# Sinkhorn attention followed by a SwiGLU FFN: attention pieces threaded through the FFN in written order, the transposing V copies moved to ScalarE, and unread matmuls in TensorE's early gaps

## The chip, the cores and the metric

One core of a Trainium2 chip. The time is device time in microseconds, the median of several executions.

Engine names: PE is TensorE's matmuls and PEld its weight loads, DVE is VectorE, ACT is ScalarE, POOL is GpSimd. PSUM is the memory into which this kernel's matmuls write; a drain is a copy out of it. A unit is the attention of two heads over four blocks (scores, Exp, AV, division, transpose); a batch has eight, and four of them make the input of one FFN half.

## The reference

Four batches, eight heads, 768 tokens, head size 64; an FFN from 512 to 1536 and back over 3072 tokens.

```python
P = sort_net                                     # (4, 8, 8, 8)
for _ in range(5):                               # Sinkhorn
    P = exp(P - max(P, -1));  P /= sum(P, -1) + 1e-9;  P /= sum(P, -2) + 1e-9
k_sorted = einsum('bhij,bhjcd->bhicd', P, k_blocks)      # 8 blocks of 96 tokens
v_sorted = einsum('bhij,bhjcd->bhicd', P, v_blocks)
attn = softmax(q_block @ k_sorted.T / 8)                 # within each block
x = (attn @ v_sorted)                                    # -> (3072, 512)
g = x @ w_gate
out = (g * sigmoid(g) * (x @ w_val)) @ w_out
```

## The kernel before

K, Q and V arrive with (head, block) on the partitions, so that the sorting is a matmul by a small mixing matrix made from P. For V the weights of such a matmul are all 96 tokens of one d, which lie 64 elements apart in the loaded tile. So V is first copied into `vch`, with d and token exchanged:

```python
def emit_vch(pair):                                  # 4 copies, 128 partitions x 1536
    for s in range(4):
        cs = slice(s * (C // 4), (s + 1) * (C // 4))
        eng = nc.gpsimd if pair else nc.vector
        eng.tensor_copy(vch[:, :, cs], nat[:, cs, :].transpose([0, 2, 1]))

def emit_att(b):
    kqt = emit_kq(b)                     # 12 chunks of 16 matmuls, PSUM drained by DVE and ACT in turn
    ...                                  # 8 units: scores, Exp, AV, divide, transpose
            if b % 2 == 0: vts[b // 2] = emit_v(b // 2)      # V of two batches at once

emit_att(0)
for b in range(B):
    if b + 1 < B:
        emit_att(b + 1)
    emit_gv(b, 0); emit_gv(b, 1)         # FFN: gate and value, per half batch (384 tokens)
    emit_out(b, 0); emit_out(b, 1)
```

The FFN step for one 128-wide slice m of the hidden layer ties three engines together. The four `g_ps` and four `v_ps` matmuls need PSUM buffers ("gen", three of them), which come free only after ScalarE's tanh and VectorE's two multiplications:

```python
th_sb = tanh(g_ps / 2)                    # ACT
gs_sb = (th_sb + 1) * g_ps                # DVE
h     = (v_ps * 0.5) * gs_sb              # DVE
```

The order on every engine is the scheduler's.

The softmax here doesn't subtract the row's maximum and nothing guards it: scores larger than these inputs give would overflow.

## Time and profile before

| | |
|---|---|
| time | 285.56 us when the prediction was made, 285.91 us with a fourth run (the profile is of one of 287.63 us, span 285.9) |
| TensorE busy | 90% of the span |
| first `h` begun (last step of the first FFN slice) | 45.64 us |
| half-rate TensorE clock after 35 us | 17.1 us |
| gaps of TensorE over 0.3 us after 35 us | 2.5 us |

The page's busy times and, of its rows of 40 equal slices, those of TensorE and ScalarE and of the granted clock (in tenths; 5 is half rate), kernel before:

```profile
PE 257.2 (90%) x2600; PEld 152.7 (53%) x2608; DVE 178.9 (63%) x383; ACT 121.7 (43%) x246; POOL 39.1 (14%) x51
...
PE   0077799969999999999999999999999999999993
...
ACT  2036745437633215976534215764332134343211
...
PEclk9999955979999999999999999999999999999999
```

TensorE is full from slice 10 on. What could be won lies in front: hardly a matmul in the first two slices, then thin ones, then slices at half clock. The chain of waits of the kernel before, as shares of the span by engine:

```profile
PE 82%; DVE 11%; ACT 3%; issue 2%; ACTq 0%
```

In stretches (columns: stretch; its length and PE busy; then PEld, DVE, ACT and POOL busy with instruction counts; granted clock; DMA share and GB/s), kernel before:

```profile
35.60:49.20 13.60, 13.36 (x116) 7.14 (x111) 7.24 (x17) 6.50 (x15) 2.94 (x6) 0.50 1.13 209
57.40:59.90 2.50, 0.00 (x0) 0.00 (x0) 0.42 (x1) 0.06 (x1) 0.00 (x0) 0.93 1.04 213
...
65.00:100.00 35.00, 34.90 (x307) 20.64 (x307) 26.61 (x56) 16.39 (x37) 10.60 (x4) 1.00 0.25 56
```

The first FFN work runs at clock 0.50, and a later pause waits for a load (Q's second half for batch 1 landed at 59.60 us, and TensorE went on at 59.90). The transposing copies of the kernel before, by group and form (line, engine, operation, count; then busy us and mean ns; then idle time before them):

```profile
L204 POOL COPY vch<-v 128x1536 bf16<-128x1536 bf16 x4 | 11.2, 2878 | 0.0
...
L204 DVE COPY vch<-v 128x1536 bf16<-128x1536 bf16 x4 | 6.0, 1490 | 0.0
```

### The profile page before, as it was taken

To read this page: it belongs to the slowest core of one execution; us is meant where nothing else is said; L and a number is where in the kernel's file an instruction comes from. 1 tells how busy PE (TensorE), PEld (TensorE's weight loads), DVE (VectorE), ACT (ScalarE), POOL (GpSimd) and SP (SyncE) were. 2 spreads that over 40 slices of the span, in tenths; PEclk is the share of its full clock that TensorE was granted. 3 is DMA by queue.
4 is the path that set the end of the run, shared out by engine and by line. 5 is a ranking of instruction groups with operands and counts; after the bars stand their busy time and mean duration, and the time that the engine had idled before them with its cause. 6 is when DMAs were issued, how large, how long until landed. Compare 5 with 4: busy or idle time off the path is not lost.

```text
span 285.9 us, 6221 instructions
## 1 busy us (share of the span) xinstructions
PE 257.2 (90%) x2600; PEld 152.7 (53%) x2608; DVE 178.9 (63%) x383; ACT 121.7 (43%) x246; POOL 39.1 (14%) x51
## 2 busy tenths in 40 slices
PE   0077799969999999999999999999999999999993
PEld 0066555746655446666655446666555445555441
DVE  6798746937988205789988304699885018888300
ACT  2036745437633215976534215764332134343211
POOL 8557421029500000000000000000000000000000
PEclk9999955979999999999999999999999999999999
DMA  6999999999100122000000122000000220000021
GB/s 99 198 203 197 200 213 204 220 214 214 38 0 1 39 110 76 2 2 0 3 0 2 38 110 76 2 2 2 0 0 2 111 102 10 0 0 3 37 110 73
DMA packets 13659, 20.84 MB, mean 73 GB/s; under 512 B 1088, under 2 KB 8768, under 8 KB 13632
## 3 DMA queue, kind: packets, MB, share of 16 engines
q0 software_dynamic: 10128, 14.16, 28.2%
q1 hardware_dynamic: 3504, 6.30, 5.8%
q8 instruction: 20, 0.33, 0.4%
q14 instruction: 7, 0.06, 0.1%
HBM read 28.32 MB, written 6.29 MB: 121 GB/s over the span
## 4 chain that ended last, share of the span: by engine, by line
PE 82%; DVE 11%; ACT 3%; issue 2%; ACTq 0%
PE v_ps L297 22%; PE g_ps L288 22%; PE o_ps L308 22%; PE av_ps L245 4%; PE qk L230 4%; PE tkq L193 3%; PE x_ps L255 3%; PE tv L214 3%; DVE kqt L180 2%; DVE vch L204 1%; DVE st L251 1%; ACT vt L182 1%; DVE vt L180 1%; ACT th_sb L291 1%; DVE colred L136 0%
## 5 line engine op out<-in xcount | busy, mean ns | idle before, releaser
L288 PE MATMUL g_ps<-xt,wg_sb 128*128 128x384 bf16 x384 | 84.8, 331 | 0.2 <-DVE h L299 0.2
L297 PE MATMUL v_ps<-xt,wv_sb 128*128 128x384 bf16 x384 | 82.1, 331 | 0.0
L291 ACT ACTIVATE th_sb<-g_ps 128x384 bf16<-128x384 f32 x96 | 47.1, 491 | 63.2 <-PE g_ps L288 62.6
L293 DVE SCALAR_TENSOR_TENSOR gs_sb<-th_sb,g_ps 128x384 bf16<-128x384 bf16 x96 | 52.9, 551 | 26.9 <-ACT th_sb L291 20.9
L308 PE MATMUL o_ps<-wo_sb,h 128*128 128x512 bf16 x280 | 62.4, 379 | 0.4
L299 DVE SCALAR_TENSOR_TENSOR h<-v_ps,gs_sb 128x384 bf16<-128x384 f32 x96 | 53.1, 553 | 9.0 <-PE v_ps L297 0.8
L297 PEld LDWEIGHTS <-wv_sb 128*128 128x128 bf16 x384 | 36.8, 98 | 24.5 <-issue 0.8
L288 PEld LDWEIGHTS <-wg_sb 128*128 128x128 bf16 x384 | 36.2, 99 | 23.5 <-issue 2.3
L308 PEld LDWEIGHTS <-h 128*128 128x128 bf16 x288 | 28.2, 98 | 33.6
L180 DVE CAST kqt<-tkq 128x512 bf16<-128x512 f32 x24 | 15.9, 688 | 33.9 <-PE tkq L193 33.9
L311 ACT COPY o_sb<-o_ps 128x512 f32<-128x512 f32 x24 | 14.1, 586 | 51.4 <-PE o_ps L308 51.4
L235 ACT ACTIVATE er<-qk 96x384 bf16<-96x384 f32 x64 | 27.1, 487 | 12.2 <-PE qk L230 12.2
L193 PE MATMUL tkq<-rmix,kq 128*64 128x64 bf16 x768 | 20.3, 212 | 5.5 <-issue 2.5
L193 PEld LDWEIGHTS <-kq 128*64 128x64 bf16 x768 | 17.7, 126 | 8.9 <-issue 7.9
L251 DVE TENSOR_TENSOR st<-av_ps,r_sb 96x512 bf16<-96x512 f32 x32 | 21.9, 684 | 0.8
L182 ACT CAST kqt<-tkq 128x512 bf16<-128x512 f32 x24 | 14.1, 586 | 15.7 <-PE tkq L193 15.6
L230 PE MATMUL qk<-kqt 64*128 64x96 bf16 x256 | 14.0, 217 | 1.9 <-DVE kqt L180 1.4
L245 PE MATMUL av_ps<-vt,er 96*128 96x65 bf16 x256 | 14.9, 202 | 0.2 <-ACT vt L182 0.2
L180 DVE CAST vt<-tv 96x512 bf16<-96x512 f32 x16 | 12.2, 785 | 2.7 <-PE tv L214 2.5
L182 ACT CAST vt<-tv 96x512 bf16<-96x512 f32 x16 | 12.5, 787 | 2.1 <-PE tv L214 1.8
L214 PE MATMUL tv<-vmix,vch 128*128 128x128 bf16 x128 | 12.4, 236 | 1.0 <-DVE vt L180 0.3
L255 PEld LDWEIGHTS <-st 96*128 96x128 bf16 x128 | 7.6, 101 | 10.5 <-DVE st L251 9.1
(43 smaller groups left out, 123.0 us busy)
## 6 DMA issues: line engine op xcount, KB each, us to landing
out_dram<-o_sb SPq DMA_DIRECT2D x24, 256.0 KB, 2.0
v<-in_v_dram POOLq DMA_DIRECT2D x8, 384.0 KB, 13.1
kq<-in_k_dram POOLq DMA_DIRECT2D x6, 384.0 KB, 11.6
kq<-in_q_dram POOLq DMA_DIRECT2D x6, 384.0 KB, 12.1
wg_sb<-in_moe_w_gate_dram POOLq DMA_DIRECT2D x6, 256.0 KB, 11.8
wv_sb<-in_moe_w_val_dram POOLq DMA_DIRECT2D x6, 256.0 KB, 11.1
wo_sb<-in_moe_w_out_dram POOLq DMA_DIRECT2D x1, 1536.0 KB, 18.9
kq<-in_k_dram POOLq DMA_DIRECT2D x4, 192.0 KB, 5.6
```

Of the source, the lines that this page charges most:

```text
L180: nc.vector.tensor_copy(dst, src)
L182: nc.scalar.copy(dst, src)
L193: nc.tensor.matmul(tp[two * D:(two + 1) * D, lc, :], lhsT=nat[:, cb * 8 + lc, :], rhs=rm[:, two, :], start=True, stop=True)
L230: nc.tensor.matmul(pss[two][:, i4, :], lhsT=flat[lo:lo + D, at:at + 128], rhs=kqt[lo:lo + D, 1, g, i, :], start=True, stop=True)
L235: nc.scalar.activation(e[:, 0:4 * C], pss[two][0:C].rearrange("p a c -> p (a c)"), AF.Exp, scale=scale)
L245: nc.tensor.matmul(av[:, two, i4, :], lhsT=es[two][:, i4 * C:i4 * C + 128], rhs=vt[:, 2 * g + two, half * 4 + i4, :], start=True, stop=True)
L288: nc.tensor.matmul(g_ps, lhsT=wg_sb[:, kc, ts(m, 128)], rhs=xt[:, kc, :], start=(kc == 0), stop=(kc == NKC - 1))
L291: nc.scalar.activation(th_sb, g_ps, AF.Tanh, scale=0.5)
L293: nc.vector.scalar_tensor_tensor(gs_sb, th_sb, 1.0, g_ps, op0=ALU.add, op1=ALU.mult)
L297: nc.tensor.matmul(v_ps, lhsT=wv_sb[:, kc, ts(m, 128)], rhs=xt[:, kc, :], start=(kc == 0), stop=(kc == NKC - 1))
L299: nc.vector.scalar_tensor_tensor(h_w[:, m, :], v_ps, 0.5, gs_sb, op0=ALU.mult, op1=ALU.mult)
L308: nc.tensor.matmul(o_ps, lhsT=h_w[:, m, ts(t3, 128)], rhs=wo_sb[:, m, :], start=(m == 0), stop=(m == NFC - 1))
```

## The change

Its intent is to start the FFN as soon as half of batch 0 is through attention, to spread the rest of attention over the first seven of the eight FFN halves so that TensorE always has dense work, and to keep its clock up by matmuls that nobody reads. All engines follow the written order in the prologue; TensorE and GpSimd also do so afterwards. The core of the diff (cut):

```diff
+    man = tc.manual_schedule(engines={ET.PE, ET.Pool, ET.DVE, ET.Activation})
     for it in range(N_ITER):
         nc.scalar.activation(p_sb, p_sb, AF.Exp)
+        if it >= 2:
+            copy_v(nc.scalar, 0, lowr, it - 2)      # vch copy, 64 x 1536, between two Exp
 ...
+    copy_v(nc.scalar, 0, lowr, 3)
+    warm(lowr, v_tiles[0]..., 4); warm(highr, kq_tiles[0]..., 4); warm(both, kq_tiles[0]..., 5)
+    ...                                             # w_ps, V of batch 0 alone (8 chunks), K/Q (12)
+    for u in range(4):                              # 4 of 8 units, with 16 unread matmuls between
+        qk(0, u); warm(both, kqts[0][:, 0:512], 2, warm_ps)
+        ...
+    man = tc.manual_schedule(engines={ET.PE, ET.Pool})
+    def copies(pair, rows, count):
+        return [(0.0, lambda s=s: copy_v(nc.scalar, pair, rows, s, count)) for s in range(count)]
+    merge(ffn(0), units(0, range(4, 8)) + mingle(kqs(1), copies(0, highr, 8)))
+    merge(ffn(1), [v_chunk(1, db, "s", "att") ...] + units(1, range(4)))
+    merge(ffn(2), mingle(units(1, range(4, 8)) + kqs(2), copies(1, slice(0, 128), 8)))
+    merge(ffn(3), [v_pair_chunk(1, db, "s", "att") ...] + units(2, range(4)))
+    merge(ffn(4), units(2, range(4, 8)) + kqs(3))
+    merge(ffn(5), units(3, range(4)));  merge(ffn(6), units(3, range(4, 8)));  merge(ffn(7), [])
-    emit_att(0) ... emit_gv ... emit_out            # the loop shown above
```

`merge` puts a few pieces of attention after each FFN slice. `ffn(n)` holds the 12 slices of half n and the output matmuls of half n-1.

## The prediction

> **What bounds it now.** TensorE. The page's busy table gives PE 90% of the span, and the chain of waits is 82% PE, nearly all FFN matmuls. Read by stages (windows, timeline), the 285.9 us are:
>
> - 0 to 36.0: PE does no FFN work. Sinkhorn ends at 11.9, first attention matmul 14.4; VectorE spends 6.0 us on four vch copies (1.49 us each) inside the kq stage, and both batches' V are mixed (16 drains of 0.79 us) before FFN starts.
> - 35.6 to 49.2 and 59.8 to 62.5: granted clock 0.50; consecutive 128x384 matmuls start 0.32 us apart instead of 0.163. Half of 16.3 us is lost, about 8 us. The Trainium skill (TensorE: Matmul & The Clock Gate, Part 1) says that an idle window drops the clock to half; this trace agrees: PE was 8% busy at 34-35 and idle at 57.4-59.9.
> - 57.4 to 59.9: PE idle ("issue"), batch 1's second K/Q half not landed: 2.5 us.
> - From there PE is nearly full; after the last matmul (281.3) 4.6 us of drain and store.
>
> Warm costs from the timeline: one FFN half 23.6 us (12 x 1.32 + 3 x 2.58), all eight 189; one attention unit (scores, AV, transpose) 0.80 us of PE; one kq chunk 0.29 to 0.36 us; V mixing 3.5 to 4 us per pair. Estimate of PE work after FFN start: about 229 us.
>
> **What changes.** (1) vch copies go to ScalarE (four of about 1.4 us, in Sinkhorn's gaps); V of batch 0 alone is mixed first, in 8 chunks. (2) FFN starts after four units instead of after the whole of batch 0; all other attention work is threaded between FFN groups in written order, its drains mostly on ScalarE. (3) 13 early unread matmuls plus about 17 between the first units keep the clock up. They cost some PE time, mostly in waits. The work in total is unchanged; only place and clock are.
>
> **New prologue (estimate).** Loads run at about 0.2 MB/us bf16 (windows): V0 lands near 7, K/Q 0 near 15.4. Early unread matmuls end near 13; w_ps about 13.5; V chunks 14.4 to 17.6; kq 17.6 to 22.5; four units, paced by VectorE (0.20+0.68+0.36 us) and start-up latency, about 7 us: FFN starts near 30, warm.
>
> **Sum.** 30 + 229 + 4.6 = 264. Add 6 to 7 us: in FFN half 0 ScalarE has about 24 us of work (12 tanh, 8 exp, 12 kq drains, 8 copies) against 23 us of PE, and V of batch 1 lands only near 42.6, so ScalarE's copies may hold up tanh; elsewhere PE in written order waits now and then for a drain. Prediction 270 us, range 262 to 278. Gain: 6 us earlier start, 8 clock, 2.5 stall, less deferred and new waits.
>
> **What would show it.** FFN's first g_ps near 30 (right) or after 33 (wrong). No 0.50 clock after FFN starts; kq chunks at 20-23 us near 21 ns a matmul, not 31. PE 97% busy or more from 30 on. If ScalarE binds, waits of g_ps or tkq for ScalarE (copies, tanh) show in FFN half 0, between 36 and 46. FFN halves 5 to 7 at 27 us or less.
>
> **What would make it wrong.** The clock falls anyway (unread matmuls too sparse, or a stall near 40 us): +4 to 7. ScalarE's copies wait for V inside Sinkhorn and delay it. In-order PE blocks on drains at each of some 150 threaded pieces: 0.1 us each is 15 us, which would leave the gain below 2%. If none of that happens, 263.
>
> Chances: faster 0.90, same 0.08, slower 0.02.

## The result and the profile after

The changed kernel takes 295.10 us (four runs, 294.79 to 296.67) against 285.91: ratio 1.033, 95% interval 1.028 to 1.039. It is slower, where 270 us was expected.

The same parts of the page, changed kernel:

```profile
PE 260.2 (89%) x2701; PEld 149.1 (51%) x2701; DVE 154.3 (53%) x351; ACT 162.7 (55%) x281; POOL 18.6 (6%) x34
...
PE   0867975599988799899989998999999999999994
...
ACT  4976459976599645454887444455443353333311
...
PEclk9999999789999799999999999999999999999999
...
PE 76%; ACT 14%; DVE 5%; issue 3%; DMA 1%; ACTq 0%
```

TensorE is no fuller than before. In slices 7 and 8 and again around 12 and 13 it has holes, and there ScalarE is at 9. In the chain of waits ScalarE rose from 3% to 14%. The groups show what it does there:

```profile
L111 ACT COPY vch<-v 128x768 bf16<-128x768 bf16 x8 | 12.0, 1538 | 0.0
L111 ACT COPY vch<-v 64x768 bf16<-64x768 bf16 x8 | 11.6, 1497 | 0.1
...
L111 ACT COPY vch<-v 64x1536 bf16<-64x1536 bf16 x4 | 11.1, 2786 | 0.0
```

The prediction had 1.4 us for the 1536-element copy; it takes 2.79, nearly twice what VectorE took before. How this hurts is seen in time order in the prologue, ScalarE alone (columns: start, duration, engine, line, operation; in brackets the idle time before it and what ended it):

```profile
5.95 0.26 ACT L163 ACTIVATE p_sb<-p_sb 32x64 f32<-32x64 f32 x1 [1.50 <-DVE p_sb L177]
6.13 2.80 ACT L111 COPY vch<-v 64x1536 bf16<-64x1536 bf16 x1
8.83 0.25 ACT L163 ACTIVATE p_sb<-p_sb 32x64 f32<-32x64 f32 x1
8.99 2.78 ACT L111 COPY vch<-v 64x1536 bf16<-64x1536 bf16 x1
11.67 0.25 ACT L163 ACTIVATE p_sb<-p_sb 32x64 f32<-32x64 f32 x1
11.83 5.48 ACT L111 COPY vch<-v 64x1536 bf16<-64x1536 bf16 x2
```

The gap between two Exp was 1.50 us, so a copy of 2.8 delays each following Exp, and the last copy ends at 17.3. TensorE waits for it before V's first matmul:

```profile
14.11 0.61 PE L349 MATMUL w_ps<-ident,p_bf 32*64 32x32 bf16 x16
...
17.36 0.87 PE L232 MATMUL tv<-vmix,vch 64*128 64x64 bf16 x13 [2.64 <-ACT vch L111]
```

And in FFN half 0, all engines between 47.5 and 53.2 us (weight loads left out):

```profile
47.58 4.29 ACT L111 COPY vch<-v 64x768 bf16<-64x768 bf16 x3
...
49.02 0.82 PE L307 MATMUL g_ps<-xt,wg_sb 128*128 128x384 bf16 x4
...
51.89 0.49 ACT L310 ACTIVATE th_sb<-g_ps 128x384 bf16<-128x384 f32 x1
...
52.41 0.56 DVE L312 SCALAR_TENSOR_TENSOR gs_sb<-th_sb,g_ps 128x384 bf16<-128x384 bf16 x1 [4.18 <-ACT th_sb L310]
...
53.02 0.65 PE L316 MATMUL v_ps<-xt,wv_sb 128*128 128x384 bf16 x3 [3.17 <-DVE gs_sb L312]
```

The gate matmuls end near 49.8. Their tanh has to stand behind a row of copies on ScalarE until 51.9; VectorE waits for the tanh, the PSUM buffer stays taken, and TensorE stands still for 3.17 us. Soon after, from 54.4 to 61.3 us, the trace's clock records show half rate. The Trainium skill (TensorE: Matmul & The Clock Gate, Part 1) says that an idle window of the activity monitor does that; both half-rate stretches after 35 us (the other is 98.8 to 102.2) follow holes here. But the stretches before them were not empty: the lengths of these clock records are multiples of 3.41 us, and in the last 3.41 us before each drop TensorE was busy for 1.42 and 1.38 us.

Three of TensorE's longest waits in the changed kernel, by place (columns: who waited for whom; us in total, times, longest):

```profile
PE v_ps L316 <- DVE gs_sb L312: 6.1, 4, 3.2
PE av_ps L277 <- DVE st L283: 6.1, 6, 1.4
...
PE g_ps L307 <- ACT o_sb L329: 2.2, 1, 2.2
```

The first and the last lead to ScalarE, by way of the tanh and of the output's drain (one of the four at v_ps, 1.4 us, stays when the copies leave ScalarE); the second is another matter, as rival B below says.

For a comparison of all kernels I use three numbers that I worked out from each trace: when the first `h` is begun, the sum of TensorE's gaps over 0.3 us after 35 us, and the half-rate time after 35 us.

| | time | first h | gaps | half rate |
|---|---|---|---|---|
| before | 285.9 | 45.6 | 2.5 | 17.1 |
| changed | 295.1 | 37.4 | 15.3 | 10.2 |

So the change did start the FFN earlier, by 8 us at the first `h`, and part of the half-rate time went. But work is deferred with that, and 13 us of new gaps follow.

### The profile page after: what moved, and what is told of

It reads as the page before. It is cut to its first block, busy times and chain, and to the rows that moved or that the text cites. A ratio compares the mean times of both kernels' runs of the same rounds, so it can differ in the third digit from the quotient of the medians.

```text
span 293.6 us, 6359 instructions
## 1 busy us (share of the span) xinstructions
PE 260.2 (89%) x2701; PEld 149.1 (51%) x2701; DVE 154.3 (53%) x351; ACT 162.7 (55%) x281; POOL 18.6 (6%) x34
## 4 chain that ended last, share of the span: by engine, by line
PE 76%; ACT 14%; DVE 5%; issue 3%; DMA 1%; ACTq 0%
PE o_ps L326 21%; PE g_ps L307 20%; PE v_ps L316 20%; ACT vch L111 9%; PE tkq L220 5%; PE av_ps L277 3%; PE qk L257 3%; PE tv L232 2%; PE x_ps L294 2%; ACT e_all L264 2%; ACT th_sb L310 1%; PE warm_ps L339 1%; DVE st L283 1%; ACT vt L189 1%; DVE gs_sb L312 1%
## 5 line engine op out<-in xcount | busy, mean ns | idle before, releaser
L307 PE MATMUL g_ps<-xt,wg_sb 128*128 128x384 bf16 x384 | 80.9, 333 | 2.2 <-ACT o_sb L329 2.2
L310 ACT ACTIVATE th_sb<-g_ps 128x384 bf16<-128x384 f32 x96 | 47.5, 495 | 41.1 <-PE g_ps L307 40.3
L326 PE MATMUL o_ps<-wo_sb,h 128*128 128x512 bf16 x288 | 65.7, 380 | 0.0
L316 PEld LDWEIGHTS <-wv_sb 128*128 128x128 bf16 x384 | 37.9, 99 | 34.2 <-issue 10.2
L111 ACT COPY vch<-v 64x768 bf16<-64x768 bf16 (+2 forms) x20 | 34.7, 1771 | 0.1
L264 ACT ACTIVATE e_all<-qk 96x384 bf16<-96x384 f32 x64 | 27.8, 486 | 11.1 <-PE qk L257 10.9
L189 ACT CAST kqt<-tkq 128x512 bf16<-128x512 f32 x42 | 23.3, 591 | 11.5 <-PE tkq L220 11.5
L189 ACT CAST vt<-tv 96x512 bf16<-96x512 f32 x28 | 19.3, 746 | 4.1 <-PE tv L232 3.3
L277 PE MATMUL av_ps<-vt,e_all 96*128 96x65 bf16 x256 | 13.7, 196 | 6.2 <-DVE st L283 6.1
L281 DVE RECIPROCAL r_sb<-av_ps 96x8 f32<-96x8 f32 x32 | 6.4, 200 | 21.8 <-PE av_ps L277 21.8
L277 PEld LDWEIGHTS <-e_all 96*128 96x128 bf16 x256 | 11.6, 99 | 12.1 <-DVE st L283 3.8
L257 PEld LDWEIGHTS <-kqt 64*128 64x128 bf16 x256 | 6.6, 94 | 9.6 <-issue 7.9
```

Of the source, the lines that this page charges most:

```text
L111: eng.copy(dst, src)
L189: nc.scalar.copy(dst, src)
L257: nc.tensor.matmul(pss[two][:, i4, :], lhsT=flat[lo:lo + D, at:at + 128], rhs=flat[lo:lo + D, GI * C + at:GI * C + at + C], start=True, st ...
L264: nc.scalar.activation(e[:, 0:4 * C], pss[two][0:C].rearrange("p a c -> p (a c)"), AF.Exp, scale=scale)
L277: nc.tensor.matmul(o[:, two, i4, :], lhsT=e[:, i4 * C:i4 * C + 128], rhs=vt[:, 2 * g + two, half * 4 + i4, :], start=True, stop=True)
L307: nc.tensor.matmul(g_ps, lhsT=wg_sb[:, kc, ts(m, 128)], rhs=xt[:, kc, :], start=(kc == 0), stop=(kc == NKC - 1))
```

## The experiments

Theory A: ScalarE's transposing copies are the cause, in the prologue and in FFN halves 0 and 1. Rival B: the written order on TensorE stalls it by itself, whoever copies, because an in-order engine waits at each threaded piece. Rival C, for the prologue: loads and unread matmuls pace it.

### What the copy costs by itself: copy_forms

```diff
+        if pair == 0 and n == 8:                      # iterate in source order
+            dst = vch3[rows, :, cs].transpose([0, 2, 1]);  src = v_tiles[pair][rows, cs, :]
+        if pair == 1:                                 # contiguous both ways: wrong result on purpose
+            dst = vch[rows, s * m:(s + 1) * m]
+            src = v_tiles[pair][rows, cs, :].rearrange("p c d -> p (c d)")
```

> Measures the copy by itself, in place; results are wrong on purpose. The changed kernel, where the four prologue copies (64x1536) stay as they are (read strided by 128 bytes, written in runs), the eight of batch 1 (64x768) run in source order (read contiguous, written strided), and the eight of pair 1 (128x768) read and write contiguously. Theory A1 (a strided bf16 read is what costs ScalarE 1.7 ns an element): contiguous ones take 0.80 to 0.85 us, source order the same or between. Rival A2 (ScalarE copies SBUF to SBUF at 1.7 ns an element in any layout): all 768-element ones take 1.5 us.

Its groups by form:

```profile
L118 ACT COPY vch<-v 64x768 bf16<-64x768 bf16 x8 | 31.5, 4203 | 0.1
...
L118 ACT COPY vch<-v 64x1536 bf16<-64x1536 bf16 x4 | 11.0, 2784 | 0.0
...
L118 ACT COPY vch<-v 128x768 bf16<-128x768 bf16 x8 | 6.8, 847 | 0.0
```

Contiguous, 768 elements take 0.85 us; read at a stride of 128 bytes 1.50 (above); written at a stride of 192 bytes 4.20. So it is the layout that costs, as A1 says; my guess for source order was wrong by far, since a strided write is the worst. From 1.497 and 2.786 us the strided read comes to (2786 - 1497) / 768 = 1.68 ns an element. The Trainium skill states both halves of this: 186 ns and 0.833 ns an element for an ACTIVATE with immediate scale and bias (ScalarE: Activation LUTs, What ACT_TABLE_LOAD costs), as an estimate from that page 826 ns for 768 elements, which fits the contiguous 847 ns, and a penalty for each access that crosses to a new 16-byte line (SBUF — State Buffer, Door 1: The DMA port swizzle), which fits ScalarE's strided forms. VectorE's transposing copy of 1536 took 1.49 us, 0.97 ns an element; whether VectorE pays for the stride too is not shown, since no run times its contiguous copy. (Time of this one, a single run with wrong results: 311.26 us.)

### The FFN's copies on VectorE: ffn_copies_on_dve

```diff
-        return [(0.0, lambda s=s: copy_v(nc.scalar, pair, rows, s, count)) for s in range(count)]
+        return [(0.0, lambda s=s: copy_v(nc.vector, pair, rows, s, count)) for s in range(count)]
```

> The changed kernel with its 16 vch copies of the FFN part (8 for batch 1, 8 for pair 1) on VectorE instead of ScalarE; the four of the prologue stay. Theory A (ScalarE is the limit of FFN halves 0 and 1, because a transposed 768-element copy takes 1.5 us there): halves 0 and 1, now about 36 and 37 us, fall to 25-29 and 31-33, no half-rate clock after 36 us, time about 278 to 282. Rival B (written PE order with threaded attention stalls by itself, whoever copies): both halves stay within 3 us of what they were, time 291 or more. On VectorE a 64x768 copy should take about 0.75 us.

286.63 us, ratio to before 0.997 (0.992 to 1.002). The 64x768 copies take 0.82 us each. From the first `h` of one half to that of the next, half 0 shrank from 34.2 to 29.4 us and half 1 from 37.0 to 31.5; no half-rate clock is left after 23.4 us; gaps fell from 15.3 to 9.2. So theory A carries 8.5 us by the medians (10.5 by the ratios, which compare runs of the same rounds), about all of the loss. copy_forms shows the same with the copies still on ScalarE: its half 1, with contiguous copies, took 30.3 us instead of 37.0, and its half 0, with copies of 4.2 us, 55.2 instead of 34.2, with one gap of TensorE of 15.4 us and then half clock. But here half 0 stayed just above A's range, and the time is above the 282 that A allowed: something else holds TensorE.

### No copy at all: no_prologue_copies and no_copies

V's matmuls take the loaded tile as it is, with a stationary operand of 96 columns 64 elements apart; in the first kernel for batch 0 only, in the second everywhere.

```diff
-            nc.tensor.matmul(tp[:, ld, :], lhsT=vch[rows, at:at + 128], rhs=mix, ...)
+            nc.tensor.matmul(tp[0:C, ld, :], lhsT=v_tiles[b // 2][rows, :, db * 8 + ld], rhs=mix, ...)
```

> The changed kernel, but batch 0's V is mixed straight from the loaded tile (stationary operand read with a stride of 64 elements, 96 columns), so the prologue has no vch copies; the FFN copies stay on ScalarE. Theory A (copies of 2.8 us hold Exp of Sinkhorn up and then V): Sinkhorn's last step ends near 11.0 instead of 13.2, V chunks start near 15 instead of 17.4, FFN starts 2 to 3 us earlier than 34.6, time about 292. If strided weights load slowly (0.2 us or more a piece), V's 64 matmuls take 13 us instead of 3.6 and nothing is gained. Rival B (prologue is paced by loads or unread matmuls): FFN start moves by less than 1 us.

> The changed kernel with no vch copy at all: V is mixed from the loaded tiles by strided stationary operands throughout, vch is gone, two buffers for V's loads. Theory A: the sum of both former runs, 274 to 279, clear of the kernel before (285.9) by over 2%. Rival B: 288 or more. If 64 strided weight loads per pair cost more than 0.1 us each, up to 6 us more in FFN halves 1 and 3.

300.31 us (ratio 1.046) and 300.83 us (1.047): slower still. The weight loads of no_copies:

```profile
L225 PEld LDWEIGHTS <-v 64*96 64x96 bf16 x128 | 21.5, 252 | 2.3 <-issue 2.3
...
L234 PEld LDWEIGHTS <-v 128*96 128x96 bf16 x64 | 11.2, 254 | 0.6
```

A strided load takes 252 ns against 95 to 111 from `vch`. V's 64 matmuls of batch 0 took 10.5 us instead of 3.6. My warning case came true, so these two runs say little for or against A as to time. They do say two things. In no_copies half 0 has neither copies nor strided loads, and it took 26.9 us instead of 34.2, as A says. And without the copies Sinkhorn ended at 11.6, yet w_ps still came at 14.07, since TensorE in written order first did the last five unread matmuls, which K's landing had released at 11.85 (without them, in mended_no_early_unread below, w_ps comes at 11.46). Rival C is right for w_ps, and A for V's start: 14.88 us in no_prologue_copies instead of 17.36.

### The prologue's copies split: split_prologue_copies

```diff
-        if it >= 2: copy_v(nc.scalar, 0, lowr, it - 2)        # and a fourth after the loop
+    copy_v(nc.scalar, 0, lowr, 0); copy_v(nc.scalar, 0, lowr, 1)    # after the fifth Exp
+    copy_v(nc.vector, 0, lowr, 2); copy_v(nc.vector, 0, lowr, 3)    # after p_bf
```

> On top of ffn_copies_on_dve (286.6): of the four prologue copies two run on ScalarE after the fifth Exp and two on VectorE after p_bf, so none stands between two Exp. Theory A (the fourth ScalarE copy, ending at 17.3, is what V's first matmul waits for): V chunks start at 15.0 to 15.4 instead of 17.4, first FFN matmul about 2 us earlier, time 284 to 285. Rival (loads or the clock pace the prologue): FFN start moves by less than 0.7 us.

V starts at 15.16 and the first `h` comes at 35.72, 1.95 us earlier, as A says. The time is 285.18 us, ratio 0.999: nothing gained. The earlier FFN half meets V of batch 1 before it has landed; VectorE, in order, waits with the copy, and AV with it:

```profile
44.24 0.81 DVE L113 COPY vch<-v 64x768 bf16<-64x768 bf16 x1 [1.78 <-DMA v<-in_v_dram]
```

TensorE's gap there grew from 1.68 to 3.42 us, and the clock fell to half for 3.4 us. A gain in the prologue was given back in the next stage.

### TensorE's order by the scheduler: pe_by_scheduler and change_pe_by_scheduler

```diff
-    man = tc.manual_schedule(engines={ET.PE, ET.Pool})
+    man = tc.manual_schedule(engines={ET.Pool})
```

> On top of ffn_copies_on_dve: from the first FFN step on TensorE's order is left to the scheduler instead of the written one. Rival B of the first set in its weaker form (the written order is what stalls PE, 9 us of gaps over 0.3 us after FFN starts): gaps fall to 4 us or less and the time to about 281. If the written order is not the cause, gaps and time stay within 2 us, or grow.

On ffn_copies_on_dve: 281.36 us, ratio 0.984 (0.978 to 0.989), gaps 4.0 instead of 9.2. The waits at AV are what went. With the written order:

```profile
PE av_ps L277 <- DVE st L283: 7.0, 7, 1.7
...
PE v_ps L316 <- DVE gs_sb L312: 1.4, 1, 1.4
```

and with the scheduler's:

```profile
PE v_ps L316 <- DVE gs_sb L312: 3.4, 4, 1.4
...
PE av_ps L277 <- DVE st L283: 0.9, 2, 0.6
```

(Columns: who waited for whom; us in total, times, longest.) AV has a single PSUM buffer, which VectorE must first empty; in the written order the next AV stands in front of FFN matmuls that could run. The scheduler lets those go first. So rival B holds too, for 5.3 us by the medians and 3.7 by the ratios.

> The changed kernel untouched but for one thing: after the first FFN step TensorE's order is the scheduler's; all vch copies stay on ScalarE. If the two causes found add up (ScalarE copies 8.5 us, written order 5 us), the time is about 290 and the gaps at v_ps waiting for tanh behind a ScalarE copy stay. If the written order is what makes the ScalarE copies harmful, the time falls to 283 or less, although the copies stay.

The untouched change with the scheduler's order: 290.18 us, ratio 1.011 (1.004 to 1.018). The time is as expected if the two causes add up, but the interval leaves room for some interplay, and the traces show it: half 1 stays at 36.9 us, with the 2.2 us wait for ScalarE at g_ps, while half 0 falls from 34.2 to 30.2. 7.7 us of gaps are left. In this profile the clock's first record is at 32.4 us (23.7 in the changed kernel) and the first `h` 2.3 us later, although the prologue's order is the same, so part of its time may be the clock's.

### The unread matmuls: no_late_unread, no_early_unread, mended_no_early_unread

The first two take unread matmuls out of ffn_copies_on_dve, the 16 between the units or the 13 before w_ps.

> On top of ffn_copies_on_dve: without the 16 unread matmuls among the first four units. If they hold the clock, it drops to half between 28 and 42 us for at least one window of 3.4 us, and the time is 2 to 7 us longer. If the units alone keep it, the time is equal or up to 1.5 us shorter (their own PE time, about 3.5 us, lies mostly in waits).

290.33 us, ratio 1.018 against 0.997 with them. In its stretches the clock stands at half:

```profile
30.00:35.00 5.00, 3.90 (x46) 2.64 (x46) 3.28 (x10) 1.39 (x4) 0.10 (x1) 0.50 1.18 227
35.00:40.00 5.00, 4.12 (x29) 1.93 (x30) 1.75 (x7) 2.34 (x6) 0.00 (x0) 0.50 1.04 220
```

ffn_copies_on_dve, with them, in the same stretches:

```profile
30.00:35.00 5.00, 4.54 (x64) 2.51 (x63) 3.81 (x10) 1.73 (x4) 0.48 (x1) 1.00 1.17 224
35.00:40.00 5.00, 4.36 (x50) 2.44 (x50) 2.20 (x8) 3.08 (x7) 0.00 (x0) 1.00 1.06 222
```

The late unread matmuls do what they are for.

> On top of ffn_copies_on_dve: without the 13 unread matmuls before w_ps. My reading: they buy nothing, because the clock record turns to full speed only at 23.4 us, after the V and K/Q matmuls, and V waits for a copy until 17.4 anyway: time within 1.5 us of 286.6. Rival (they are what warms the clock by 23 us): full clock comes one or two windows of 3.4 us later, K/Q chunks stay at 31 ns a matmul, FFN starts 1 to 3 us later.

288.63 us, ratio 1.009; its one profile shows half clock from 27.7 to 34.5. That spoke for the rival, so the question was put once more to the mended kernel of the next section, with five rounds:

> On top of all_mended_scheduled (274.3, ratio 0.958): without the 13 unread matmuls before w_ps. V's first matmul stays at 15.0 to 15.3, since its copies end at 15.1, so only the clock can change. If the early unread matmuls help the clock, as the 288.6 of no_early_unread against 286.6 hinted, half clock lasts 3 to 7 us longer before 36 us and the time is 275.5 to 278, ratio 0.962 to 0.97. If they only fill a wait, the ratio stays within 0.954 to 0.962.

274.55 us, ratio 0.961 (0.957 to 0.965), against 0.958 (0.954 to 0.963) with them. V starts at 15.16, as before. The intervals overlap; in this one's profile the clock was at full rate from 21.6 us on. The runs fall in two groups of three, near 273.5 (granted clock 0.998 to 1.000) and 275.7 (0.987 to 0.988), so the groups differ by the clock. Whether the early ones help the clock on average is not settled; the intervals exclude that they are worth much more than 1%.

### The mends together: all_mended_scheduled and all_mended_written

Prologue copies split as above, the FFN part's copies on GpSimd, the scheduler's order for TensorE; the second kernel keeps the written order and lets units and K/Q chunks alternate in halves 2 and 4.

```diff
-        return [(0.0, lambda s=s: copy_v(nc.scalar, pair, rows, s, count)) for s in range(count)]
+        return [(0.0, lambda s=s: copy_v(nc.gpsimd, pair, rows, s, count)) for s in range(count)]
```

> The changed kernel with the three mends together: prologue copies split between ScalarE and VectorE after the fifth Exp, the FFN part's copies on GpSimd (idle then; about 1.5 us for 64x768 and 128x768), TensorE's order from the first FFN step by the scheduler. FFN starts near 33, no VectorE wait for V's landing, gaps after FFN start 3 us or less: time 276 to 280, faster than the kernel before by 2% or slightly more. If GpSimd's copies slow VectorE down, its 553 ns scalar_tensor_tensor grow and the time is 281 or more.

> As all_mended_scheduled, but TensorE keeps the written order, with units and K/Q chunks alternating in FFN halves 2 and 4, where they came one after the other before: the 1.1 us waits for AV's single PSUM buffer at the end of those halves vanish, half 0 keeps its two (3 us). Time 279 to 283, 2 to 4 us longer than with the scheduler's order.

274.28 us, ratio 0.958 (0.954 to 0.963): faster than both kernels. With the written order 279.94 us, ratio 0.977 (0.972 to 0.982). The page of all_mended_scheduled:

```profile
PE 254.5 (93%) x2679; PEld 147.8 (54%) x2701; DVE 156.0 (57%) x353; ACT 135.0 (50%) x263; POOL 43.9 (16%) x50
...
PE   0796999999999999999899999999999999999993
...
PEclk9998899999999999999999999999999999999999
```

and its groups by form:

```profile
L319 DVE SCALAR_TENSOR_TENSOR h<-v_ps,gs_sb 128x384 bf16<-128x384 f32 x96 | 53.3, 555 | 7.2
...
L113 POOL COPY vch<-v 64x768 bf16<-64x768 bf16 x8 | 11.8, 1516 | 16.2 <-DMA v<-in_v_dram 16.2
L113 POOL COPY vch<-v 128x768 bf16<-128x768 bf16 x8 | 11.7, 1507 | 15.3 <-PE av_ps L278 15.3
```

GpSimd needs as long as ScalarE did, 1.5 us, but nobody stands behind it; it also does the waiting for V's landing (16.2 us), which had stopped VectorE in the split kernel. VectorE's own instructions kept their length (555 ns, as in the changed kernel). TensorE's gaps after 35 us came down to 0.5 us.

| | time | ratio | first h | gaps | half rate |
|---|---|---|---|---|---|
| changed | 295.1 | 1.033 | 37.4 | 15.3 | 10.2 |
| change_pe_by_scheduler | 290.2 | 1.011 | 39.7 | 7.7 | 6.8 |
| ffn_copies_on_dve | 286.6 | 0.997 | 37.7 | 9.2 | 0 |
| split_prologue_copies | 285.2 | 0.999 | 35.7 | 10.9 | 3.4 |
| pe_by_scheduler | 281.4 | 0.984 | 37.7 | 4.0 | 0 |
| all_mended_written | 279.9 | 0.977 | 37.0 | 4.7 | 0 |
| all_mended_scheduled | 274.3 | 0.958 | 36.7 | 0.5 | 0 |

Of these only all_mended_scheduled is faster than the kernel before by clearly more than 2%; the intervals of pe_by_scheduler and all_mended_written reach across that line. Time follows the gaps and the half-rate time more than it does the FFN's start. Moving the FFN copies from VectorE to GpSimd was not run alone, so its share of the last step is not separated from the interplay with the split.

## Why the prediction was wrong

- **"PE" bounds the kernel before, the losses lie before 63 us**: right; from 65 to 100 us TensorE was busy for 34.90 of 35.00 us, so the mended kernel's 4% comes from before.
- **"vch copies go to ScalarE (four of about 1.4 us, in Sinkhorn's gaps)"**: this step failed. They took 2.79 us. I had taken ScalarE's rate from drains that read PSUM (0.59 us for 128x512) and VectorE's 1.49 us for the transposing copy, and assumed that a transposed read costs ScalarE nothing extra. V started at 17.4 instead of 14.4, and the first complete FFN group ended at 36.2 (its first matmul started at 32.7 and the group waited for the rest of x), not near 30.
- **"in FFN half 0 ScalarE has about 24 us of work ... against 23 us of PE ... Add 6 to 7 us"**: the mechanism was right, and the size was not. The eight copies took 12.0 us (8 x 1.50) instead of the 7.1 that the other terms leave of the 24 (12 tanh of 0.49, 8 Exp of 0.49, 12 drains of 0.59), so the sum is about 29 us. The other eight, written for half 2, ran on ScalarE from 82.6 us on and did the same to half 1; all 20 copies together took 34.7 us. Taking the 16 FFN copies off ScalarE gave back 8.5 us, more than the 6 to 7 that were set aside for all waits. The cause that I named beside it, V landing late (42.6 predicted; it landed at 43.8), did not bind in the changed kernel; it did as soon as the prologue was 2 us shorter.
- **"PE in written order waits now and then for a drain"** was inside those 6 to 7 us. It cost 4 to 5 us by itself (286.6 against 281.4; 3.7 by the ratios), mostly at AV's single PSUM buffer. I had the case in the list of what would make it wrong, in the milder form of 0.1 us a piece. The waits were few and long (seven of up to 1.7 us).
- **"Gain: ... 8 clock"**: failed. Half rate after 35 us fell from 17.1 to 10.2 only, because the new stalls let the clock fall again. With the copies off ScalarE it was gone, and removing the late unread matmuls brought it back. The early unread matmuls did not do what was predicted either: from 20 to 23 us TensorE ran 98 matmuls in 3.00 us, 31 ns each and not 21, and the first full-rate record is at 23.7.
- **"FFN halves 5 to 7 at 27 us or less"**: halves 5 and 6, which have neither copies nor K/Q chunks, took 26.8 us each, which is the predicted 23.6 and four units of 0.80. What was wrong is mostly what the other engines let TensorE do.
- The mended kernel, without the two mis-sized terms, stands at 274.3 us, inside the predicted range of 262 to 278. It is a different kernel, so it does not make the prediction right, and that it lies in the range is partly luck. With gaps of only 0.5 us it should by the prediction's sum have taken about 264. The rest is three small misses: the first g_ps came at 31.97 us instead of 30; from there to the last matmul (267.98) it was 236.0 us instead of 229, TensorE being busy for 233.8 of them; and the device time is 1.8 us longer than the profiled span (274.27 and 272.5).

## What to carry to other kernels

Before work moves to another engine, measure that same access pattern on that engine: a copy with a 128-byte stride cost ScalarE 1.8 times its contiguous self, and a strided write five times, while VectorE did the strided read of 1536 in 1.49 us where ScalarE took 2.79. An engine that answers TensorE within a short loop (here tanh, between two PSUM buffers) should not get long work that could run elsewhere; put it on an engine behind which nothing waits, even a slow one. In a written order, an instruction that needs a single-buffered PSUM tile should have dense work in front of it, not behind it; and after each mend look at the next stage, since a shorter prologue alone gave nothing back.

## What the Trainium skill lacked or had wrong

- SBUF — State Buffer (Door 1: The DMA port swizzle) gives the 16-byte lines and a penalty, without its size on ScalarE or VectorE. Here ScalarE paid 1.68 ns an element for bf16 read at 128 bytes, and 4.20 us for 768 elements written at 192 bytes (5.0 times the contiguous 0.847 us); VectorE's transposed read took 0.97 ns an element (not compared with a contiguous one).
- ScalarE: Activation LUTs (What ACT_TABLE_LOAD costs) states 186 ns and 0.833 ns an element with no word on layout. It holds for the contiguous copy (0.847 us for 768) and not for the strided ones.
- TensorE: Matmul & The Clock Gate (LDWEIGHTS) gives columns / 1.2 ns, by which I estimate 80 ns for 96 columns. A stationary operand with columns 64 elements apart took 252 ns; no page gives the price of that stride.
- TensorE: Matmul & The Clock Gate (Part 1) speaks of at least one busy window that frees the clock. In the changed kernel 13 unread matmuls filled 8.2 to 14.2 us almost without a pause (the first eight on 64 of 128 rows), and the trace's first clock record (full) is at 23.7 us; in no_prologue_copies and all_mended_written it came at 13.9. The profile's clock row shows full rate before the first record, although nine unread 512-column matmuls then took 4.13 us. The page does not say how little work counts as idle: here the clock fell after 3.41 us with 1.42 and with 1.38 us of TensorE work.
- I found no figure for GpSimd's transposing copy on any page (GPSIMD Engine Reference, Performance pitfalls for Q7 kernels, has a cost of strided reads, for kernels written for its cores): 1.51 us for 64x768 and 128x768, beside VectorE instructions that stayed at 555 ns.
